# One VectorE multiply in place of two ScalarE activations that normalise the attention result of a head pair

## The chip, the cores and the metric

The kernel runs on one core of a Trainium2 chip. The core has five engines that each take their instructions strictly in the order in which they stand: TensorE (PE in the profile, PEld for its weight loads), VectorE (DVE), ScalarE (ACT), GpSimd (POOL) and SyncE (SP, which here only issues DMAs). They wait for one another by semaphores. The metric is the device time of one execution in microseconds (us); lower is better.

## The reference

The program computes attention with a top-k mask, then a dense layer, then a layer of experts. What matters here is the first part:

```
scores = scale * (q @ k^T)                    # 4 batches, 8 heads, 576 tokens, 64 per head
kth    = 32nd largest of each row
attn   = exp(where(scores >= kth, scores, -1e9) - max)
attn   = attn / (sum(attn) + 1e-9)            # the division of this case
x      = attn @ v                             # then heads side by side: 2304 tokens x 512
h      = softplus(x @ w_in); x2 = h @ w_out   # dense layer, 512 -> 2048 -> 512
out    = gate * (relu(x2 @ w1[e]) @ w2[e])    # each token by its one expert e of 8
```

The kernel does not divide the weights. It multiplies the unnormalised weights by v, with a column of ones beside v so that the sums come out as a 65th column, and divides the result.

## The kernel before, in words

The program has two parts. Part one does the attention, the dense layer and the routing of each token to its expert; part two does the experts.

Attention goes in 72 groups of two score tiles. A score tile is 128 queries (or twice 64, called the tail) of one head against all 576 keys. For a group, TensorE writes scores into two PSUM tiles, `sa` and `sb`, one buffer each (L401); ScalarE copies both to SBUF as `s` (L411, L447); VectorE reads `sb` and `s` and finds the 32 largest values of each row (L441 to L446 fold the row into shorter candidate lists, L451 to L467 pick eight at a time, in place); ScalarE and GpSimd make the masked exponentials `e` (L477 to L479); ScalarE and GpSimd split `e` into two 16-bit halves `p` (L487 to L489); SyncE issues a DMA that transposes `p` into `pT` (L491). `p` has two buffers.

Three groups later `emit_av` multiplies `pT` by v (L506, L508) into the PSUM tile `m`. `m` has one buffer and holds both heads of a pair, each with 64 results and its sum. When the second head is done, VectorE makes `rc`, the reciprocal of the two sums (L530, L532), and the two heads are multiplied by it into `x` (L534). This happens 80 times: 64 times for 128 queries, 16 times for the 64 of a tail. Only then may TensorE write `m` for the next pair. When all four head pairs of some tokens are in `x`, `unit_x` splits it into 16-bit halves (ScalarE L553, GpSimd L554) and transposes it by DMA; the dense layer (L593, L607, L608, L633) runs on it in between the attention groups. The weights of the dense layer are decoded in the first 300 us on ScalarE, VectorE and GpSimd (L243 to L256).

The order on each engine is not written by hand. A scheduler places the instructions by its own estimate of when each can start, with priorities given in the code (`tc.high_priority`), so that a change of one instruction can shift its neighbours on all engines. The matmuls of `emit_av` are to be issued behind the next group's score matmuls (L822). The program holds a second copy of part one for unusual inputs; it does not run here, and it has the same lines.

Of the kernel before, what the change touches and what calls it, by code (L numbers as in the profile page):

```python
# [13 lines left out]
AF = mybir.ActivationFunctionType  # L14
ALU = mybir.AluOpType
# [4 lines left out]
B, H, S, D = 4, 8, 576, 64  # L20
# [176 lines left out]
def part_one(tc, ctx, q, k, v, w_in, w_out, const, ident, before, ones, iota_e, reg_e, wg, ids,  # L197
             ohcum, done, early, table, rows, flags, sums, w_sums, e_sums, kths):
    nc = tc.nc
# [294 lines left out]
    def x_tile(key):  # L494
        if key not in x_t:
            x_t[key] = xp.tile([128, NP, 2, D], F32, name=f"x{key[1]}", bufs=XB if isinstance(key[1], int) else 1)
        return x_t[key]

    def emit_av(m, kind):
        b, hp = pairs[m]  # L500
        v16, sc = pair[m][3:5]
        pT = pt_t.pop((m, kind))
        def products(o, pT, h):
            for r in range(R):
                c = r if r < 5 else r - 5
                nc.tensor.matmul(o[:, h, 0:D + 1], lhsT=pT(r), rhs=v16[:, h, c, 0:D + 1], start=r == 0, stop=r == R - 1)  # L506
                if r < 5:
                    nc.tensor.matmul(o[:, h, 0:D], lhsT=pT(r), rhs=v16[:, h, c, D + 2:], start=False, stop=False)  # L508

        def out_tile():  # L510
            return ps_m.tile([128, 512], F32, name="m")[:, :2 * D + 4].rearrange("p (h c) -> p h c", h=2)

        if kind == "tail":
            o = out_tile()
            p0 = 64 * (b % 2)
            for h in range(2):
                products(o[p0:p0 + 64], lambda r: pT[:, r, h * 64:h * 64 + 64], h)
            xt, ps_ = x_tile((b // 2, "tail%d" % (b // 2))), slice(p0, p0 + 64)
        else:
            t, h = kind  # L520
            if h == 0:
                o_t[m, t] = out_tile()
            o = o_t[m, t]
            products(o, lambda r: pT[:, r, :], h)
            if h == 0:
                return
            del o_t[m, t]
            xt, ps_ = x_tile((b, t)), slice(0, 128)
        rc = sm.tile([128, 2, 1], F32, name="rc")
        nc.vector.tensor_scalar(rc[ps_], o[ps_, :, D:D + 1], ESC * 1e-9,  # L530
                                2.0 ** -X_UP if flags is not None else sc[ps_, 2:3], op0=ALU.add, op1=ALU.mult)
        nc.vector.reciprocal(rc[ps_], rc[ps_])  # L532
        for h in range(2):
            nc.scalar.activation(xt[ps_, hp, h], o[ps_, h, 0:D], AF.Copy, scale=rc[ps_, h])  # L534


    def unit_x(tiles):
# [250 lines left out]
    for i in range(-1, n + LAG):  # L788
# [29 lines left out]
        if j >= 0:  # L818
            with tc.high_priority(offset=A_AV), ExitStack() as behind_scores:
                if i + 1 < n:  # L820

                    behind_scores.enter_context(tc.issue_after(last_qk[0].ins))  # L822
                for x in groups[j]:
                    emit_av(*x)
            for u in units.get(j, []):
                started += 1
                ready.append((u, started))
# [274 lines left out]
```

## Time and profile before

| | us |
|---|---|
| time, median of 3 runs (lowest to highest) | 1096.41 (1095.99 to 1100.68) |
| time of the profiled execution | 1104.11 |
| its span, from the first to the last instruction | 1102.3 |
| its mean granted TensorE clock | 0.925 of full speed |

The profile records each instruction of one execution with its start and its length. "Busy" counts the time in which an engine had an instruction under way; instructions of one engine may overlap, so that the time from one start to the next is often shorter than the length of one. "Idle" times name the instruction whose end released the waiting engine. The chain of waits goes back from the last instruction to what released it, and so on to the start. The profiled execution took 7.7 us more than the median; all sums are made as differences in it and then carried to the median.

### The profile page before, as it was taken

How to read it: one execution, taken by the hardware profiler on the slowest of the kernel's cores; microseconds unless marked ns; L12 is line 12 of the kernel's file. 1: busy time of each engine (PE TensorE's matmuls, PEld its weight loads, DVE VectorE, ACT ScalarE, POOL GpSimd, SP SyncE). 2: the span in 40 equal slices, each digit the busy share in tenths (PEclk: the TensorE clock that was granted, in tenths of full speed). 3: DMA queues.
4: the chain of work that ended last, by engine and by line, in shares of the span. 5: the costliest groups of instructions: out<-in, count | busy, mean ns of one | idle time of the engine just before them, and what ended most of it. 6: DMA issues, size and time to landing. Idle time of an engine off the chain costs nothing.

```text
span 1102.3 us, 22261 instructions
## 1 busy us (share of the span) xinstructions
PE 900.3 (82%) x7146; PEld 664.0 (60%) x7146; DVE 852.6 (77%) x2921; ACT 833.1 (76%) x2026; POOL 603.8 (55%) x631
## 2 busy tenths in 40 slices
PE   1124359675978978799989799998999999999995
PEld 0012246344655655666556566666688899999993
DVE  3898999699966847889889799982445897777774
ACT  4889899798868867989897898994478655555553
POOL 2788898798656756767776877773101011211111
PEclk9976569876988989899999999999999999999998
DMA  7888898776756878867978646644601486676660
GB/s 173 202 200 182 180 205 180 164 159 129 126 77 122 143 122 119 134 76 126 139 153 124 106 79 93 86 80 67 202 1 30 99 252 205 217 245 227 228 222 23
DMA packets 295860, 156.98 MB, mean 142 GB/s; under 512 B 257524, under 2 KB 257652, under 8 KB 295732
## 3 DMA queue, kind: packets, MB, share of 16 engines
q1 hardware_dynamic: 292116, 145.73, 63.1%
q0 software_dynamic: 3616, 9.72, 2.6%
q8 instruction: 58, 0.95, 0.4%
q14 instruction: 70, 0.57, 0.2%
HBM read 77.89 MB, written 11.11 MB: 81 GB/s over the span
## 4 chain that ended last, share of the span: by engine, by line
PE 37%; DMA 19%; ACT 17%; POOL 9%; DVE 8%; issue 5%; SPq 3%; POOLq 0%; ACTq 0%; DVEq 0%
PE h L933 9%; DMA pT<-p 9%; PE y L946 9%; PE h L593 6%; PE y L633 4%; POOL p L489 3%; PE y L630 3%; ACT p L487 3%; POOL e L478 2%; DMA w<-in_moe_w_out_dram 2%; ACT e L479 2%; ACT e L477 2%; DVE mx L467 2%; DMA vn<-in_v_dram 2%; DVE wk L463 1%
## 5 line engine op out<-in xcount | busy, mean ns | idle before, releaser
L593 PE MATMUL h<-xT,w_in_s 128*128 128x256 f16 (+1 forms) x1920 | 231.8, 272 | 18.6 <-DMA xT<-xh 7.4
L633 PE MATMUL y<-w_out_s,g 128*128 128x512 f32 x480 | 233.9, 610 | 2.0 <-ACT g L608 2.0
L593 PEld LDWEIGHTS <-w_in_s 128*128 128x128 f16 x1920 | 177.0, 102 | 86.4 <-issue 53.8
L478 POOL TENSOR_TENSOR e<-s,e 128x576 f32<-128x576 f32 x144 | 204.0, 1432 | 22.1 <-ACT e L477 21.8
L467 DVE MAX8 mx<-wk 128x8 f32<-128x128 f32 (+2 forms) x432 | 201.1, 500 | 0.1
L401 PEld LDWEIGHTS <-q 128*128 128x128 f16 (+1 forms) x640 | 56.2, 109 | 195.7 <-issue 148.5
L489 POOL TENSOR_TENSOR p<-e,p 128x512 f16<-128x512 f32 x144 | 167.3, 1162 | 0.0
L463 DVE MATCH_REPLACE8 wk<-mx,wk 128x128 f32<-128x128 f32 (+1 forms) x432 | 144.4, 340 | 0.0
L487 ACT ACTIVATE p<-e 128x576 f16<-128x576 f32 x144 | 97.9, 683 | 42.1 <-DMA pT<-p 41.3
L401 PE MATMUL sa<-kt,q 128*128 128x256 f16 (+1 forms) x320 | 52.9, 304 | 86.7 <-ACT s L411 35.2
L633 PEld LDWEIGHTS y<-w_out_s,g 128*128 128x128 f32 x480 | 83.4, 194 | 62.4 <-issue 57.4
L913 POOL DMA_INDIRECT out_dram<-ot,idx x19 | 19.6, 1030 | 176.3 <-DVE ot L912 156.5
L479 ACT ACTIVATE e<-e,bias 128x576 f32<-128x576 f32 x144 | 111.0, 772 | 6.1 <-POOL e L478 5.9
L401 PE MATMUL sb<-kt,q 128*128 128x320 f16 (+1 forms) x320 | 63.6, 342 | 63.4 <-ACT s L447 63.4
L933 PEld LDWEIGHTS h<-xT,wf 128*128 128x128 f32 x864 | 111.9, 191 | 5.3 <-ACT wf L894 0.2
L933 PE MATMUL h<-xT,wf 128*128 128x256 f32 x864 | 114.0, 283 | 0.0
L946 PE MATMUL y<-wf,hT 128*128 128x512 f32 x432 | 112.9, 399 | 0.3 <-DVE ds L690 0.3
L477 ACT ACTIVATE e<-s,kths 128x576 f32<-128x576 f32 x144 | 106.2, 770 | 1.2 <-POOL p L489 0.4
L506 PE MATMUL m<-v,pT 128*128 128x65 f16 (+1 forms) x1440 | 96.0, 203 | 8.1 <-ACT xtail L534 6.8
L488 POOL TENSOR_TENSOR p<-e,p 128x64 f16<-128x64 f32 x144 | 45.6, 317 | 96.4 <-ACT p L487 80.9
L506 PEld LDWEIGHTS <-pT 128*128 128x128 f16 (+1 forms) x1440 | 89.5, 107 | 14.2 <-issue 10.9
L441 DVE TENSOR_TENSOR sb<-sb,s 128x256 f32<-128x256 f32 x72 | 30.6, 425 | 73.0 <-ACT s L411 48.9
(204 smaller groups left out, 1885.5 us busy)
## 6 DMA issues: line engine op xcount, KB each, us to landing
w1r<-in_moe_w_dram SPq DMA_DIRECT2D x20, 1024.0 KB, 6.0
w2r<-in_moe_w_dram SPq DMA_DIRECT2D x20, 1024.0 KB, 7.7
w<-in_moe_w_in_dram SPq DMA_DIRECT2D x16, 512.0 KB, 5.1
w<-in_moe_w_out_dram SPq DMA_DIRECT2D x16, 512.0 KB, 4.2
rows<-xr SPq DMA_DIRECT2D x37, 128.2 KB, 2.4
qn<-in_q_dram SPq DMA_DIRECT2D x16, 288.0 KB, 3.4
kn<-in_k_dram SPq DMA_DIRECT2D x16, 288.0 KB, 3.2
vn<-in_v_dram SPq DMA_DIRECT2D x16, 288.0 KB, 3.7
```

The source lines that it names most:

```text
L401: last_qk[0] = nc.tensor.matmul(ps[p0:p1], lhsT=qs[:, h, r0:r1, :].rearrange("p r d -> p (r d)"), rhs=kt[:, k0:k1, cs], start=first, stop= ...
L463: nc.vector.match_replace(out=to, in_to_replace=mx[:, i, 8 * j:8 * j + 8], in_values=src[i], imm_value=NEG)
L467: nc.vector.max(out=mx[:, i, 8 * j + 8:8 * j + 16], in_=src[i])
L478: nc.gpsimd.tensor_tensor(out=e[i], in0=s[i], in1=e[i], op=ALU.subtract)
L479: nc.scalar.activation(e[i], e[i], AF.Exp, bias=bt[:, i], scale=SCORE)
L487: nc.scalar.activation(p16[:, 0:S], e[i], AF.Copy)
L489: nc.gpsimd.tensor_tensor(out=p16[:, S + D:], in0=e[i][:, 0:S - D], in1=p16[:, 0:S - D], op=ALU.subtract)
L506: nc.tensor.matmul(o[:, h, 0:D + 1], lhsT=pT(r), rhs=v16[:, h, c, 0:D + 1], start=r == 0, stop=r == R - 1)
L593: nc.tensor.matmul(hps[:, :n], lhsT=w_in_s[:, c, j, p, o:o + 128], rhs=xT[:, 0:len(u.tiles), r, c, :], start=m == 0, stop=m == 3 * KD - 1)
L633: nc.tensor.matmul(u.y[i], lhsT=g[:, cs], rhs=w_out_s[:, f, :], start=f == 0, stop=f == KF - 1)
L933: nc.tensor.matmul(h, lhsT=w1f[:, a, c, :], rhs=xT[:, b, c, :], start=n == 0, stop=n == 3 * KD - 1)
L946: nc.tensor.matmul(y[i], lhsT=hT[g][:, a, i * 128:i * 128 + 128], rhs=w2f[:, b, :], start=g == 0 and n == 0, stop=g == KF2 - 1 and n == 2)
```

## The change

Two ScalarE instructions (one for each head, 128 x 64 elements from PSUM, scaled by that head's reciprocal) are taken out. One VectorE instruction over both heads (128 x 2 x 64 elements from PSUM, times `rc` repeated along the row) takes their place. It does the same arithmetic.

```
-        for h in range(2):
-            nc.scalar.activation(xt[ps_, hp, h], o[ps_, h, 0:D], AF.Copy, scale=rc[ps_, h])
+        nc.vector.tensor_tensor(out=xt[ps_, hp], in0=o[ps_, :, 0:D],
+                                in1=rc[ps_].to_broadcast([ps_.stop - ps_.start, 2, D]), op=ALU.mult)
```

The new instruction has line 533. In the orders below, names are those of the code (`rc`, `m`, `sb`, `s`, `gt`, `wk`, `xh` as above; `x` with a number is one tile of `x`), and a row is one instruction, or several alike with their count. First VectorE, at the second head pair of the first batch, near the start of the program. Before:

```order
L467 MAX mx<-wk 128x8 x2
L530 TENSOR_SCALAR rc<-m 128x2
L532 RECIPROCAL rc<-rc 128x2
L441 TENSOR_TENSOR sb<-sb,s 128x2x128
L442 TENSOR_TENSOR gt<-sb,s 128x256
L443 TENSOR_TENSOR wk<-sb,gt 128x2x128
```

And in the changed kernel:

```order
L467 MAX mx<-wk 128x8 x2
L530 TENSOR_SCALAR rc<-m 128x2
L532 RECIPROCAL rc<-rc 128x2
L441 TENSOR_TENSOR sb<-sb,s 128x2x128
L533 TENSOR_TENSOR x_922<-m,rc 128x128
L442 TENSOR_TENSOR gt<-sb,s 128x256
L443 TENSOR_TENSOR wk<-sb,gt 128x2x128
```

The multiply stands behind L441, the first instruction of the next group's search, which itself waits for scores. Second, ScalarE, where the first finished tile of `x` is split for the dense layer (with what each row waits for in brackets). Before:

```order
L534 ACTIVATE x_789<-m,rc 128x64 [waits DVE_49,PE_49]
L534 ACTIVATE x_789<-m,rc 128x64
L477 ACTIVATE e<-s,kths 128x576 [waits Activation_49]
L477 ACTIVATE e<-s,kths 128x576 [waits Pool_49]
L243 ACTIVATE xr<-w 128x512 [waits DMAHW2_49]
L247 ACTIVATE w<-w 128x512
L553 ACTIVATE xh<-x_789 128x512 [waits Activation_49]
L447 ACTIVATE s<-sb 128x2x320 [waits DVE_49]
```

And in the changed kernel:

```order
L243 ACTIVATE xr<-w 128x512 [waits DMAHW1_49,Pool_49]
L247 ACTIVATE w<-w 128x512
L476 ACTIVATE kths<-mx 128x2 [waits DVE_49]
L477 ACTIVATE e<-s,kths 128x576 [waits Activation_49]
L477 ACTIVATE e<-s,kths 128x576 [waits Pool_49]
L553 ACTIVATE xh<-x_789 128x512 [waits DVE_49]
L447 ACTIVATE s<-sb 128x2x320 [waits DVE_49,PE_49]
```

The two activations are gone from ScalarE's row, and the split L553, which waited for ScalarE's own work, waits for VectorE.

## Rows read from the trace of the kernel before

**Rows 1.** Busy time by stretch; columns as the first row says.
```profile
core 0: us, PE busy (x) PEld busy (x) DVE busy (x) ACT busy (x) POOL busy (x), PEclk, DMA share, GB/s
55.00:770.00 715.00, 574.08 (x4998) 385.99 (x4999) 599.03 (x2226) 602.99 (x1502) 529.68 (x548) 0.89 0.72 130
770.00:1102.00 332.00, 317.37 (x2118) 273.79 (x2116) 220.69 (x593) 192.95 (x448) 44.69 (x43) 0.99 0.51 162
```
**Rows 2.** Chain that ended last, shares of the whole span by engine.
```profile
PE 37%; DMA 19%; ACT 17%; POOL 9%; DVE 8%; issue 5%; SPq 3%; POOLq 0%; ACTq 0%; DVEq 0%
```
**Rows 3.** The chain from 770 us to the end, by line.
```profile
by line: PE h L933 31.3%; PE y L946 30.2%; PE h L593 11.4%; PE y L630 10.4%; PE y L633 3.1%; PE tp L903 2.5%; PE h L961 1.6%; PE h L667 1.2%; PE y L978 1.0%; PE h L661 0.7%; ACT wf L894 0.4%; issue 0.4%; PE h L688 0.3%; DVE wf L895 0.3%; AC
```
**Rows 4.** Who waited for whom: us in total, times, longest.
```profile
DVE sb L441 <- ACT s L411: 48.9, 23, 11.4
DVE sb L441 <- PE sb L401: 22.9, 10, 8.4
PE sb L401 <- ACT s L447: 63.4, 20, 6.7
ACT p L487 <- DMA pT<-p: 41.3, 19, 8.0
DVE rc L530 <- PE m L506: 23.2, 13, 5.4
ACT x L534 <- DVE rc L532: 7.6, 5, 3.2
```
**Rows 5.** ScalarE's groups by form: line, shapes, count, busy us, mean ns.
```profile
L534 ACT ACTIVATE x<-m,rc 128x64 f32<-128x64 f32 x128 | 32.6, 307 | 10.6 <-DVE rc L532 7.6 <-DVE sf L1011 2.5 <-PE h L593 0.4
L534 ACT ACTIVATE xtail<-m,rc 64x64 f32<-64x64 f32 x32 | 8.1, 303 | 0.2
```
**Rows 6.** ScalarE's timeline around two pairs: start us, us, instruction.
```profile
520.11 0.53 ACT L534 ACTIVATE x<-m,rc 128x64 f32<-128x64 f32 x2
520.50 0.80 ACT L477 ACTIVATE e<-s,kths 128x576 f32<-128x576 f32 x1
...
694.97 0.51 ACT L534 ACTIVATE xtail<-m,rc 64x64 f32<-64x64 f32 x2
695.50 0.70 ACT L447 ACTIVATE s<-sb 128x640 f32<-128x640 f32 x1
```
**Rows 7.** VectorE's groups by form, as Rows 5.
```profile
L441 DVE TENSOR_TENSOR sb<-sb,s 128x256 f32<-128x256 f32 x72 | 30.6, 425 | 73.0 <-ACT s L411 48.9 <-PE sb L401 22.9 <-ACT x2T L663 1.2
L445 DVE COPY wk<-sb 128x128 f32<-128x128 f32 x72 | 20.1, 279 | 0.0
L470 DVE TENSOR_TENSOR flags<-mx 128x16 f32<-128x16 f32 x18 | 15.7, 870 | 0.3
L530 DVE TENSOR_SCALAR rc<-m 128x2 f32<-128x2 f32 x64 | 9.5, 148 | 18.9 <-PE m L506 18.9
```
**Rows 8.** VectorE's timeline inside one search.
```profile
460.95 0.28 DVE L445 COPY wk<-sb 128x128 f32<-128x128 f32 x1
461.15 0.68 DVE L446 TENSOR_TENSOR wk<-sb,s 128x512 f32<-128x512 f32 x1
```
**Rows 9.** Single lines of VectorE: shortest, median and longest instruction in ns.
```profile
L470 DVE TENSOR_TENSOR flags<-mx x18: 177/454/3612, 63.7 to 740.0; 128x16 f32<-128x16 f32 x18
L441 DVE TENSOR_TENSOR sb<-sb,s x72: 404/432/433, 22.4 to 731.6; 128x256 f32<-128x256 f32 x72
```
**Rows 10.** VectorE's timeline where L441 stands between L530 and L532.
```profile
528.34 0.14 DVE L530 TENSOR_SCALAR rc<-m 64x2 f32<-64x2 f32 x1
532.00 0.43 DVE L441 TENSOR_TENSOR sb<-sb,s 128x256 f32<-128x256 f32 x1 [3.51 <-ACT s L411]
532.34 0.14 DVE L532 RECIPROCAL rc<-rc 64x2 f32<-64x2 f32 x1
```
**Rows 11.** Line 534 alone: who waited for it (us, times).
```profile
PE m L506: 8.1, 9
```

## The prediction

> **What bounds the kernel now.** I read the busy times by stretch first. From 55 to 770 us, while attention runs, VectorE is busy 599.0 of 715 us and ScalarE 603.0, both 84%; TensorE is at 574.1 and GpSimd at 529.7 [rows 1]. No engine is full, and the two between which work is moved are equally loaded. After 770 us attention is over, and the changed lines no longer run. The chain shows who sets the end: over the whole span 17% of it is ScalarE and 8% VectorE, 19% DMA [rows 2]. From 770 us on it is matmuls almost alone, with 0.4% for ScalarE and 0.3% for VectorE in the largest groups shown [rows 3], so that nearly all of ScalarE's and VectorE's shares lie before, and the last 332 us should keep their length. Third, the waits. VectorE's largest is at L441, the first step of a search: 48.9 us for ScalarE's copy L411 and 22.9 us for TensorE's scores [rows 4], and TensorE in turn stands 63.4 us in front of `sb` until ScalarE has emptied it with L447 [rows 4]. So ScalarE is late for VectorE more than the other way round. ScalarE's own largest wait in attention is for the transposing DMA of `p`, 41.3 us [rows 4]: there it has nothing to do, and a lighter ScalarE only waits longer.
>
> **What the change removes.** 160 activations on ScalarE, 40.7 us by the two groups (32.6 + 8.1) [rows 5]. Their mean lengths are 307 and 303 ns, so that two one after the other would be 0.61 us, but they overlap: a pair takes 0.53 us, and the next instruction starts 0.39 us after the pair did in the one place and 0.53 us in the other [rows 6]. Times 80 that is 31 or 42 us; I take the middle, 36 us. The Trainium skill (ScalarE: Activation LUTs, "What ACT_TABLE_LOAD costs") says that back-to-back activations overlap by about 93 ns; by it a pair costs less than its two lengths, and the trace agrees, since 0.61 less 0.53 us is 0.08 us. ScalarE also loses 7.6 us of waiting for `rc` [rows 4], and TensorE 8.1 us of waiting for L534 to free `m` [rows 11]; I count neither, since the new instruction puts waits of its own in their place.
>
> **What it adds.** 80 VectorE instructions, each over 128 elements from PSUM. The nearest row is L445, a copy of 128 x 128 elements out of PSUM, 279 ns long [rows 7], whose successor starts 0.20 us after it [rows 8]. 14 of the 80 stand directly behind the reciprocal that they wait for and are charged the whole 0.279 us, 66 stand elsewhere and are charged 0.20 us: 3.9 + 13.2 = 17 us. The lower bound is the short L530 at 148 ns, 80 times, 12 us [rows 7]; the upper one is L470, the only row with an operand repeated along the row, 870 ns mean, 70 us [rows 7]. I keep near L445, because L470 is not long by nature: its shortest is 177 ns and its longest 3612, while L441, which reads PSUM and SBUF as the new instruction does, never leaves 404 to 433 ns [rows 9]. The Trainium skill (GPSIMD Engine Reference, "Specifications") says that GpSimd contends with VectorE for SBUF where a VectorE instruction has two SBUF inputs. L470 has two and is stretched, L441 has one and is not, so the trace agrees; by that rule the new instruction stays short, by the mean of L470 alone it would be a rival, below. [...]
>
> **What it moves.** The scheduler shifts work on all engines after the first head pairs. Counted in the two orders, the progress of the dense layer against attention is alike: with the 40th of the 80 results multiplied both have issued 48 blocks of its first layer, with the last one 122. The transposes and loads stand at nearly the same places in SyncE's queue, the subtractions in GpSimd's. I take nothing for this, and 10 us either way for the range: the longest single waits at L441 are 11.4 and 8.4 us [rows 4], so that one group more or less that comes so badly placed is worth that much. Two waits change hands. TensorE's first matmul into `m` waits for VectorE and not for ScalarE; behind it in TensorE's row stand the dense layer's matmuls and the next scores. And 16 of the 18 splits L553 wait for VectorE, where before ScalarE's own order was enough; behind a split stands for example L447, for which VectorE's next L441 waits. A split costs nothing where the last multiply is long done. As an upper bound each could wait as long as L441 does on average, (48.9 + 22.9) / 33 = 2.2 us [rows 4]: 18 times, 39 us on ScalarE. I take 0, because the multiply stands rows ahead of the split in the order.
>
> **The sum.** Not every us of an engine is on the chain. ScalarE's 17% of 1102.3 us is 187 us, 0.31 of its 603 busy us; VectorE's 8% is 88 us, 0.15 of its 599 [rows 1, 2]. 36 us less on ScalarE at 0.31 are -11.2 us; 17 us more on VectorE at 0.15 are +2.6 us. Together -8.6 us: 1104.1 becomes 1095.5 for the profiled execution, and the median 1096.4 becomes 1088.
>
> **The rivals.**
> - *Hidden anyway.* ScalarE's relief goes into its 41.3 us of waiting for the transposes [rows 4], whose DMAs come no sooner. 19% of the chain being DMA speaks for it [rows 2]; that only part of these waits is at the places where the activations stood speaks against it. The gain is nothing, VectorE's 2.6 us remain, and the shifted order is left as the only other difference: 1097 us.
> - *The multiply held behind L441.* In the new order L441 stands between L530 and the multiply 17 times; before, it stood between L530 and the reciprocal 10 times, and then `rc` came late: at 528.34 us L530 is done, L441 waits 3.51 us for ScalarE, and L532 starts only at 532.34 [rows 10]. Until the multiply is through, `m` is not free, and TensorE holds its row. At 2.2 us each, the 7 further places give +15 us on TensorE. It decides as soon as these waits are on TensorE's path in most of the places; against it speaks that the 10 old ones cost TensorE little, 8.1 us for all waits on L534 [rows 11]. With the gain of 8.6 us off: +6.8, 1103 us. Without that gain, 1111 us, the upper part of the range.
> - *Stretched like L470.* 70 us on VectorE in place of 17. The 116 us in which VectorE is idle in attention [rows 1] could hold it, but they are waits in the middle of searches. With all of it on the path, less the 36 us of ScalarE: +34, 1130 us.
> - *ScalarE was the bound.* All 36 us come back, as VectorE's 48.9 us of waiting for L411 shrink [rows 4]; VectorE gives back its 2.6: -33, 1063 us. Two engines equally busy speak against it.
> - That the change doesn't do what it says: the 160 activations are gone from ScalarE's order, and the 80 multiplies stand in VectorE's. There is no such case to price.
>
> **How the numbers follow.** I give my forecast 0.46, the hidden gain 0.22, the held multiply 0.22, the stretched one 0.04 and the bound ScalarE 0.06. A difference under 0.5%, 5.5 us, can't be told from none here: faster is below 1090.9 us, slower above 1101.9. The forecast's own range is 1077 to 1098: the chain's shares could be wrong by half, and the order adds noise. Two thirds of it lie below 1090.9 and nearly one third between. Faster: 0.31 of the forecast, 0.06 of the bound ScalarE, 0.04 of the hidden gain and 0.03 of the held multiply, 0.44. Slower: 0.15 of the held multiply, 0.04 of the stretched, 0.05 of the hidden gain through its order, 0.02 of the forecast, 0.26. The rest, 0.30, is no difference. The range reaches down over a part of the bound ScalarE and up over both prices of the held multiply: 1072 to 1111 us.
>
> **What would show it.** L533 should be 0.28 us long (0.20 to 0.35), 80 times, 22 us by its group. ScalarE should be busy some 40 us less in attention, VectorE's waits at L441 for L411 should shrink from 48.9 us, and ScalarE's wait for the transposes should grow by less than ScalarE lost. The end of attention should come some 9 us earlier, and the last 332 us be as long as before. If the transposes' wait grows by 30 us or more, the gain was hidden; if TensorE waits for L533 much over the 8.1 us that it waited for L534, the multiply is held; if L533 is 0.5 us or longer in the mean, it is stretched. My forecast is wrong if attention ends later with L533 short and TensorE not waiting for it: then the shifted order, or VectorE's extra 17 us at full weight, cost more than ScalarE's relief is worth.

## The result, and the profile after

The changed kernel takes 1068.7 us (median of 4 runs, 1066.5 to 1074.1) against 1098.6 us (1096.0 to 1103.7) for the kernel before, on the same chip: a ratio of 0.973, 95% interval 0.970 to 0.977. That is 30 us faster, 3.5 times the predicted gain of 8.6 us, and below the predicted range. The profiled execution took 1068.5 us with a span of 1066.8. The two profiled executions lie 35.6 us apart, some 6 us more than the medians, so that the times read from the two traces below add up to 35 us and not to 30.

The granted TensorE clock is not the cause. It was 0.938 of full speed in the profiled execution after and 0.925 before; but thirteen executions of the kernel before, timed beside the experiments, had a clock of 0.934 to 0.943 and took 1091.8 to 1101.7 us.

Busy time by stretch, cut where attention ends:

```profile
core 0: us, PE busy (x) PEld busy (x) DVE busy (x) ACT busy (x) POOL busy (x), PEclk, DMA share, GB/s
55.00:735.00 680.00, 561.37 (x4998) 378.88 (x4999) 606.31 (x2306) 572.94 (x1342) 528.35 (x548) 0.91 0.73 137
735.00:1066.00 331.00, 317.47 (x2118) 273.88 (x2116) 220.75 (x593) 192.97 (x448) 44.42 (x43) 0.99 0.50 162
```

Against [rows 1] the last part is 331 us as before (332), and attention is 35 us shorter (680 against 715). ScalarE has lost 160 instructions and 30 us. VectorE has gained 80 instructions and only 7.3 us: over the whole span the new ones, which overlap their neighbours, add 13.1 us to its busy time, and its other instructions take 5.7 us less, L470 alone 4.7. The chain's shares have moved from ScalarE to VectorE [rows 2] (and the transposes of `p`, part of DMA, from 9% of the span to 4%):

```profile
PE 40%; DMA 17%; DVE 14%; ACT 13%; POOL 8%; issue 4%; SPq 3%; POOLq 0%; ACTq 0%; DVEq 0%
```

The waits that answer to [rows 4] (waiting engine and line, who ended the wait, us in total, times, longest):

```profile
PE sb L401 <- ACT s L447: 66.2, 24, 7.2
DVE sb L441 <- ACT s L411: 28.6, 19, 3.2
DVE rc L530 <- PE m L506: 20.6, 12, 4.5
ACT p L487 <- DMA pT<-p: 20.1, 18, 4.1
DVE sb L441 <- PE sb L401: 17.7, 5, 8.6
```

VectorE waits 20 us less for ScalarE's copy L411, and the longest single wait there fell from 11.4 to 3.2 us. What does not fit the prediction is the fourth row: a lighter ScalarE should have waited longer for the transposes, and it waits 20.1 us, half of the 41.3 us before. Something other than ScalarE's load made the transposes come in time (experiment 1 shows what).

The new instruction itself is as estimated (line, shapes, count, busy us, mean ns, idle before it; L470 stands with it for the last section), and its neighbour starts 0.20 us after it, as L446 does after L445 [rows 8]:

```profile
L470 DVE TENSOR_TENSOR flags<-mx 128x16 f32<-128x16 f32 x18 | 11.0, 610 | 0.1
L533 DVE TENSOR_TENSOR x<-m,rc 128x128 f32<-128x128 f32 x64 | 17.8, 279 | 0.5
L533 DVE TENSOR_TENSOR xtail<-m,rc 64x128 f32<-64x128 f32 x16 | 4.5, 283 | 0.3
```

```profile
461.17 0.28 DVE L533 TENSOR_TENSOR x<-m,rc 128x128 f32<-128x128 f32 x1
461.37 0.41 DVE L443 TENSOR_TENSOR wk<-sb,gt 128x256 f32<-128x256 f32 x1
```

TensorE's wait for it, from the answer on line 533 alone, is in the place of the 8.1 us of [rows 11]:

```profile
  PE m L506: 6.3, 4
```

To see where the 30 us arise I marked, in both timelines of VectorE, the start of the first instruction (L441) of each group's search. The groups are counted from 0:

| group | before | after | difference |
|---|---|---|---|
| 9 | 117.2 | 114.6 | -2.6 |
| 18 | 228.6 | 224.1 | -4.5 |
| 27 | 317.6 | 304.9 | -12.7 |
| 30 | 351.2 | 331.3 | -19.9 |
| 33 | 377.6 | 358.4 | -19.2 |
| 36 | 424.3 | 389.7 | -34.6 |
| 48 | 532.0 | 500.5 | -31.5 |
| 69 | 716.5 | 685.1 | -31.4 |

A relief of 0.4 us per group would give a straight line. Instead 30 of the 31 us come between groups 18 and 36, in steps, and behind group 36 nothing is gained. In the kernel before ScalarE stands still four times for over 4 us in that stretch (ScalarE's timeline; in brackets the idle time ahead of the instruction and what ended it):

```profile
308.40 0.68 ACT L487 ACTIVATE p<-e 128x576 f16<-128x576 f32 x1 [7.95 <-DMA pT<-p]
...
334.22 0.68 ACT L487 ACTIVATE p<-e 128x576 f16<-128x576 f32 x1 [4.55 <-DMA pT<-p]
...
393.10 0.68 ACT L332 ACTIVATE junk<-vn 128x576 f16<-128x576 f32 x1 [6.65 <-DMA vn<-in_v_dram]
...
421.38 0.68 ACT L487 ACTIVATE p<-e 128x576 f16<-128x576 f32 x1 [5.65 <-DMA pT<-p]
```

24.8 us in all. (L332 sums up a v tile that is to be prepared; L487 may not write `p` until an earlier `p` has been transposed.) The third shows how such a stall travels: L411 stands behind it on ScalarE, and VectorE's next search begins 11.37 us late, the longest wait at L441 in [rows 4]:

```profile
396.57 0.43 DVE L441 TENSOR_TENSOR sb<-sb,s 128x256 f32<-128x256 f32 x1 [11.37 <-ACT s L411]
```

After the change ScalarE has two waits of over 3 us between 200 and 440 us, 8.5 us in all, both for a staging buffer (L362):

```profile
375.36 0.68 ACT L362 ACTIVATE st<-kn 128x576 f16<-128x576 f32 x1 [3.31 <-DMA q<-st]
...
397.81 0.68 ACT L362 ACTIVATE st<-kn 128x576 f16<-128x576 f32 x1 [5.20 <-DMA q<-st]
```

What stands behind the first stall is seen in SyncE's queue, before:

```profile
288.14 1.14 SPq L698 DMA_DIRECT2D rows<-xr  x2
291.45 1.57 SPq L491 DMA_TRANSPOSE pT<-p  x1
293.12 1.19 SPq L714 DMA_DIRECT2D rows<-xr  x2
294.47 17.47 SPq L491 DMA_TRANSPOSE pT<-p  x3
```

and after:

```profile
281.47 1.14 SPq L698 DMA_DIRECT2D rows<-xr  x2
285.22 1.30 SPq L491 DMA_TRANSPOSE pT<-p  x1
286.62 0.53 SPq L714 DMA_DIRECT2D rows<-xr  x1
287.32 1.31 SPq L491 DMA_TRANSPOSE pT<-p  x1
288.69 0.61 SPq L714 DMA_DIRECT2D rows<-xr  x1
```

L714 writes zeros over rows of a scratch tensor. The second of the two is large; by the issues of that stretch (KB each, median us to landing):

```profile
rows<-xr SPq DMA_DIRECT2D x1, 1154.2 KB, 8.9
```

Before, both stand ahead of the transpose of the next `p`, and that transpose (the first of the three in the last row) then takes 5.03 us in the queue where the ones around it take 1.3 to 1.8, and releases ScalarE some 14 us after its issue; after, one transpose slips in between. The Trainium skill (DMA: Bandwidth & Descriptors, "Queues, rings and completion order") says that on each DMA engine the descriptors are taken in ring order; the two queues agree with it, as the transpose issued behind the large write is the late one.

### The profile page after: what moved, and what is told of

Its sections match the earlier page's. It is cut to its first block, busy times and chain, and to the rows that moved or that the text cites. A ratio compares the mean times of both kernels' runs of the same rounds, so it can differ in the third digit from the quotient of the medians.

```text
span 1066.8 us, 22144 instructions
## 1 busy us (share of the span) xinstructions
PE 887.7 (83%) x7146; PEld 656.9 (62%) x7146; DVE 860.0 (81%) x3001; ACT 802.9 (75%) x1866; POOL 602.2 (56%) x631
## 4 chain that ended last, share of the span: by engine, by line
PE 40%; DMA 17%; DVE 14%; ACT 13%; POOL 8%; issue 4%; SPq 3%; POOLq 0%; ACTq 0%; DVEq 0%
PE h L933 9%; PE y L946 8%; PE h L593 8%; PE y L633 6%; DMA pT<-p 4%; PE y L630 3%; DVE mx L467 3%; DMA w<-in_moe_w_in_dram 3%; DMA kt<-st 2%; POOL p L489 2%; DVE wk L463 2%; DMA q<-st 2%; POOL e L478 2%; DMA w<-in_moe_w_out_dram 2%; ACT e L479 2%
## 5 line engine op out<-in xcount | busy, mean ns | idle before, releaser
L633 PE MATMUL y<-w_out_s,g 128*128 128x512 f32 x480 | 230.5, 604 | 7.4 <-ACT g L608 7.2
L593 PE MATMUL h<-xT,w_in_s 128*128 128x256 f16 (+1 forms) x1920 | 225.5, 267 | 13.3 <-ACT w_in_s L255 5.3
L593 PEld LDWEIGHTS <-w_in_s 128*128 128x128 f16 x1920 | 173.5, 100 | 72.4 <-issue 42.2
L487 ACT ACTIVATE p<-e 128x576 f16<-128x576 f32 x144 | 97.3, 680 | 20.9 <-DMA pT<-p 20.1
L946 PEld LDWEIGHTS y<-wf,hT 128*128 128x128 f32 x432 | 76.7, 189 | 13.4 <-DVE ds L690 0.3
```

The costliest lines, as they stand in the source:

```text
L593: nc.tensor.matmul(hps[:, :n], lhsT=w_in_s[:, c, j, p, o:o + 128], rhs=xT[:, 0:len(u.tiles), r, c, :], start=m == 0, stop=m == 3 * KD - 1)
L633: nc.tensor.matmul(u.y[i], lhsT=g[:, cs], rhs=w_out_s[:, f, :], start=f == 0, stop=f == KF - 1)
L946: nc.tensor.matmul(y[i], lhsT=hT[g][:, a, i * 128:i * 128 + 128], rhs=w2f[:, b, :], start=g == 0 and n == 0, stop=g == KF2 - 1 and n == 2)
```

## The experiments

All but four kernels below hold every instruction to a written order: the scheduler's list of a kernel, or one put together from two of them. In the programs so built every engine's order is that of the list, but for the changes named. "Old order" is that of the kernel before, "new order" that of the changed kernel. All ratios are to the kernel before in the same runs, with 95% intervals.

**1. The exchange and the order apart.** *new_in_old_order*: the new operation in the old order, the multiply right behind its reciprocal. *old_in_new_order*: the two activations in the new order, where the multiply had been dispatched.

> The new multiply, with every other instruction of the part that runs held in the order of the kernel before; the multiply stands right behind its reciprocal. Theory A (the exchange of the operations itself gives the gain, as ScalarE was what the others waited for): 0.973 to 0.980 of the time before. Theory B (the gain is the new order that the scheduler made, above all between 284 and 424 us, where 20 to 29 of the 35 us arise): 0.992 to 1.000.

> The two activations, with every other instruction held in the order of the changed kernel; the pair stands on ScalarE where the changed kernel dispatched the multiply. Theory A: 0.995 to 1.005 of the time before, the gain gone. Theory B: 0.973 to 0.985, the gain kept.

Measured: 1.003 [1.001, 1.006] and 0.988 [0.985, 0.992]. The first lies above the ranges of both theories, the second between them. In the old order the exchange gains nothing; in the new order 13 us are there without it, and the exchange adds some 16 (0.988 to 0.973). It is the order that makes the transposes come in time: with both activations still on ScalarE, the wait for them in the new order is (old_in_new_order; its profiled execution took 1074.3 us, 12 less than its median)

```profile
ACT p L487 <- DMA pT<-p: 18.3, 17, 3.7
```

The same holds for ScalarE's waits of over 3 us between 200 and 440 us. In the old order they come to 24.8 us with the old operation and 22.0 with the new one (new_in_old_order), in the new order to 11.5 with the old one and 8.5 with the new.

**2. Which engine's load counts in the new order.** *act_filler* keeps the multiply and gives ScalarE two dead activations in place of those removed:

```
+        jk = stg.tile([128, 2, D], F16, name="jk")
+        for h in range(2):
+            nc.scalar.activation(jk[ps_, h], ident[ps_, 0:D], AF.Copy, scale=rc[ps_, h])
```

*dve_twice* does the multiply twice:

```
+        nc.vector.tensor_tensor(out=jk[ps_], in0=o[ps_, :, 0:D],
+                                in1=rc[ps_].to_broadcast([ps_.stop - ps_.start, 2, D]), op=ALU.mult)
```

> The changed kernel in its own order, and on ScalarE two activations more for each pair, over 128 x 64 elements of SBUF with a scale read from rc, whose result nobody reads: ScalarE's 36 to 42 us are back, VectorE keeps the multiply, and m is still freed by VectorE. Theory A: 0.99 to 1.005 of the time before, since ScalarE's time was the gain. Theory B: 0.973 to 0.985. If it was who frees m that counted, 0.973 too.

> The changed kernel in its own order, with the multiply done twice, the second time into a tile that nobody reads: 16 to 22 us more on VectorE, on which m is freed 0.2 us later. By the prediction's share of VectorE in the chain (0.15): +2.6 us, 0.976 of the time before. If VectorE's time is at full weight: +16 us, 0.988.

Measured: 0.986 [0.983, 0.990] and 0.977 [0.974, 0.981]. 35 us more on ScalarE (busy 837.7 against 802.9) cost 14 us, 0.4 us each; with them come 6.9 us in which ScalarE stands before a dead activation until `rc` is ready. The result lies between the ranges of the two theories. 14.5 us more on VectorE (874.5 against 860.0) cost 4 us, and the interval overlaps that of the changed kernel. So in this order ScalarE's load has a price. VectorE's is below full weight, since 0.988 lies outside the interval, but cannot be told from none, nor, us for us, from ScalarE's.

**3. Place of the multiply, place of the gain.** *old_dispatch*: the new operation in the old order, the multiply where the first activation had been dispatched. *window_new*: the same with only the instructions between the searches of groups 17 and 37 in the new order. *window_old*: the new order, with that stretch in the old one. *window_new_late*: only groups 28 to 37 in the new order.

> The new operation with every other instruction in the order of the kernel before; the multiply stands on VectorE where that order had dispatched the first of the two ScalarE operations (some instructions of other work between it and its reciprocal), no longer right behind its reciprocal as in new_in_old_order (1.0031). If new_in_old_order was flat only because VectorE stood at the multiply waiting for its reciprocal, this run gives the exchange its price: about -14 us, ratio 0.985 to 0.990. If in the old order the freed ScalarE time is worth nothing, wherever the multiply stands, the ratio is 0.997 to 1.004 and the waits of ScalarE's L487 for the transposes stay near 37 us.

> The new operation; the order of before, except that the instructions between the search of group 17 and that of group 37 (about 220 to 430 us; 2,430 of 12,216 instructions) stand in the order that the changed kernel has. If the gain is made by the order of that stretch: ratio 0.972 to 0.982, the waits of L487 for the transposes near 20 to 25 us, and the start of group 36 near 390 us. If the gain is spread over the whole order, or made by ScalarE's lighter load everywhere: 0.990 to 1.003.

> The complement: the new operation in the new order, except that the same stretch (groups 17 to 37) stands in the old order. If the stretch makes the gain: 0.995 to 1.005, with the start of group 36 near 419 to 424 us. If the gain is spread: 0.973 to 0.985.

> As window_new with only groups 28 to 37 in the new order (about 325 to 430 us). Of the 35 us, by the starts of the searches, 12 had come by group 27 and 22 came between 27 and 36. If the stretches add up: ratio 0.980 to 0.986. If the later stretch profits only where the earlier one has run ahead: 0.993 to 1.003.

Measured: 1.004 [1.001, 1.007], 0.992 [0.989, 0.995], 0.995 [0.993, 0.997] and 1.000 [0.998, 1.003]. The place of the multiply is not it; in old_dispatch the wait for the transposes, expected near 37 us, came to 51.1. Putting the stretch back into the old order takes 24 of the 29 us away; alone in the old order it gives 13 us against old_dispatch. It gave more at first: group 36 started 26 us before that of the kernel before, but group 69 only 20, and from the last search to the end window_new takes 377 us, where before takes 371 and after 365. The last nine groups alone give 4 us against old_dispatch, with intervals that overlap. So most of the gain needs the order of that stretch, but it is not a sum of pieces. My expectation of 0.972 to 0.982 for window_new was wrong.

**4. SyncE's queue alone.** In *sp_four* the new operation runs in the old order, and only SyncE's queue is changed, at four places, to what stands there in the new one. The first and the last:

```
 L714 DMA rows<-xr 64x513
-L714 DMA rows<-xr 576x1x513
 L491 DMA_TRANSPOSE pT<-p_3430
+L714 DMA rows<-xr 576x1x513
...
+L491 DMA_TRANSPOSE pT<-p_4856
 L322 DMA vn<-in_v_dram
-L322 DMA kn<-in_k_dram
 L698 DMA rows<-xr
-L698 DMA rows<-xr
-L491 DMA_TRANSPOSE pT<-p_4856
 L491 DMA_TRANSPOSE pT<-p_4862
+L322 DMA kn<-in_k_dram
+L698 DMA rows<-xr
```

*sp_all* has all of that queue's stretch in the new order, *old_op_sp_four* is the kernel before with the four places changed, and *sp_undone* is the changed kernel with the four places put back.

> As old_dispatch (new operation, order of before), except that SyncE's queue alone stands in the new order at four places, 26 of its 623 entries: the 1,154 KB zero write (L714) goes behind one transpose in place of ahead of it; a kt transpose goes ahead of two pT transposes; one k load and one row write go behind two pT transposes and the v load; and one pT transpose goes ahead of a v load, the other ahead of a k load and a row write. In the traces of the order of before, ScalarE's L487 and L332 stand 8.0, 4.6, 6.7 and 5.7 us behind these transfers (at 300, 330, 386 and 416 us). Theory Q, that these collisions in the queue are where the new order gains: the four stalls shrink by 12 to 20 us in all, ratio 0.984 to 0.992. Rival, that the order on the computing engines gains and the queue only follows: the stalls stay or are replaced, ratio 1.000 to 1.005.

> As sp_four with all of SyncE's queue between 285 and 470 us in the new order (91 entries), the other four engines as in before. Theory Q: like sp_four or better, 0.978 to 0.990. Rival (the other engines' order): 1.000 to 1.005.

> The reverse: the changed kernel with its own order, in which SyncE's queue alone stands in the order of before at the same four places. Theory Q: the stalls of ScalarE at L487 and L332 come back and it loses 12 to 20 us, ratio 0.984 to 0.992. Rival: 0.972 to 0.977, as the changed kernel.

> The kernel before, with both ScalarE operations and its own order, in which SyncE's queue alone takes the four new places. If the queue's gain is there without the exchange: 0.984 to 0.992. If ScalarE needs the time that the exchange frees before the queue can help: 0.995 to 1.003.

Measured: sp_four 0.998 [0.995, 1.001], sp_all 1.000 [0.997, 1.003], sp_undone 0.985 [0.981, 0.989], old_op_sp_four 0.996 [0.993, 0.999]. In the new order four places of one queue are worth 13 us, 0.985 against 0.973. The first stall is back (7.31 us at 301 us), and so is the last, longer than ever (ScalarE's timeline, then SyncE's queue, of sp_undone):

```profile
407.16 0.68 ACT L487 ACTIVATE p<-e 128x576 f16<-128x576 f32 x1 [11.57 <-DMA pT<-p]
```

```profile
392.43 0.34 SPq L322 DMA_DIRECT2D vn<-in_v_dram  x1
395.61 0.33 SPq L322 DMA_DIRECT2D kn<-in_k_dram  x1
396.06 1.11 SPq L698 DMA_DIRECT2D rows<-xr  x2
397.21 3.38 SPq L491 DMA_TRANSPOSE pT<-p  x2
400.69 5.73 SPq L368 DMA_TRANSPOSE q<-st  x2
```

Two loads of 288 KB and two row writes stand ahead of the two transposes, as at 408 us in the kernel before; the next `p` is held 11.57 us. Over the whole run two of its waits are those of the kernel before, although its ratio is 0.985, so that they alone do not give the time:

```profile
DVE sb L441 <- ACT s L411: 49.1, 22, 12.1
ACT p L487 <- DMA pT<-p: 42.2, 19, 11.6
```

In the old order the same four places give 6 us with the new operation (0.998 against 1.004) and 5 with the old one. sp_four lies between the ranges of theory Q and its rival. Its trace shows what is in the way: the stalls at the transposes shrank (8.0 to 3.75 us at the first, the last gone, the second as before), but ScalarE also stands at two sums over v tiles that have not landed. The first of them is the third stall of the kernel before (6.65 us there, 5.07 in old_dispatch); the second is new. The four come to 20.6 us, against 21.8 in old_dispatch:

```profile
382.99 0.68 ACT L332 ACTIVATE junk<-vn 128x576 f16<-128x576 f32 x1 [5.15 <-DMA vn<-in_v_dram]
...
408.23 0.68 ACT L332 ACTIVATE junk<-vn 128x576 f16<-128x576 f32 x1 [7.06 <-DMA vn<-in_v_dram]
```

**5. ScalarE's order, and what is left.** *act_two* is sp_four with two sums L332 moved down ScalarE's row. *six_moves* is the changed kernel with six instructions that wait there for a transfer (four L362, two L332) moved down by 3 to 8 places.

> As sp_four (new operation, order of before, four places of SyncE's queue in the new order: 0.998), and on ScalarE two sums over a v tile (L332 junk<-vn, which nothing reads soon) stand 10 and 12 instructions later, so that the loads have landed when they come up. Theory: ScalarE stands in order behind late transfers, in whatever instruction meets them, and this is what the old order loses; the two stalls (5.2 and 7.1 us) go, and the ratio is 0.985 to 0.993. Rival: the 12 us come back at another instruction, and the ratio stays at 0.996 to 1.001.

> The changed kernel in its own order, except that six instructions of ScalarE that wait there for a transfer (L362 at 336, 375, 398 and 507 us, L332 at 245 and 417 us; 16.2 us of waits in all) stand 3 to 8 instructions later. Theory: about half of these waits is won, 4 to 10 us, ratio 0.964 to 0.970. Rival: they are covered, or come back elsewhere, 0.971 to 0.978.

Measured: 0.996 [0.993, 0.998] and 0.974 [0.971, 0.978]. Of the two stalls act_two only took away the second (7.06 to 0.66 us): I had moved the sums of two neighbouring pairs of heads, and one of them was not the one that stalled at 383 us, which still waits 6.28 us. 0.996 against 0.998 is inside the intervals, so that the run neither confirms nor refutes its theory. six_moves gains nothing: the waits for the staging buffer (16.9 us in the changed kernel, 9.3 for q and 7.6 for k) are no longer among its largest, and that for the transposes has grown in their place from 20.1 to 27.3 us (ScalarE's waits in attention):

```profile
ACT p L487 <- DMA pT<-p: 27.3, 18, 5.1
```

**6. Other orders.** The scheduler made its own order here, with one number changed in both kernels: `A_PREP = 140` in place of 150 (*prep140*), or `A_SC = 95` in place of 100 (*sc95*).

> The kernel before with one number changed, A_PREP = 140 in place of 150, the lead that the scheduler's priorities give to the preparation of the next pair of heads; nothing else is changed, but the scheduler then orders the main block anew. If an order from any cause moves the time by about as much as the change did: outside 0.995 to 1.005, as low as 0.985 or as high as 1.015. If the order of the changed kernel was special: 0.996 to 1.004.

> The changed kernel with the same A_PREP = 140. If the exchange gains in any order that the scheduler makes for it: 0.970 to 0.985, and 10 us or more under before_prep140. If most of the gain was the luck of one order: 0.985 to 1.000, and within 8 us of before_prep140.

> The kernel before with A_SC = 95 in place of 100, the lead of the scores in the scheduler's priorities; nothing else is changed. If orders differ by about 1 per cent among themselves: anywhere from 0.980 to 1.012, most likely outside 0.997 to 1.003.

> The changed kernel with A_SC = 95. If the exchange gains nothing by itself and the order decides: within 12 us of before_sc95, on either side, and above 0.980. If the exchange gains as in the original pair: 20 us or more under before_sc95.

Measured: 1091.0 and 1090.6 us (0.992 [0.990, 0.995] and 0.993 [0.990, 0.996]) with A_PREP, 1091.9 and 1091.9 us (0.995 [0.993, 0.997] and 0.995 [0.993, 0.998]) with A_SC. In neither pair does the change move the time clear of the intervals, and a new order by itself moved the kernel before by 5 to 8 us. Here the two kernels of a pair have different orders, so that exchange and order are not apart: a gain of the one could be lost by the other. With A_SC = 95 the waits look like the case that the prediction called hidden: VectorE's wait for ScalarE shrinks, and ScalarE's for the transposes grows. Before and then after:

```profile
DVE sb L441 <- ACT s L411: 47.3, 21, 7.5
ACT p L487 <- DMA pT<-p: 25.1, 11, 6.4
```

```profile
ACT p L487 <- DMA pT<-p: 34.8, 15, 4.8
DVE sb L441 <- ACT s L411: 40.8, 19, 7.2
```

None of the runs is faster than the changed kernel.

## Why the prediction was wrong, point by point

- **What moved: the failed step.** The prediction looked at the orders, found that "the transposes and loads stand at nearly the same places in SyncE's queue", and went on: "I take nothing for this, and 10 us either way for the range". 71 of that queue's 623 entries had moved. The old operation in the new order gains 13 us (0.988), and four places of SyncE's queue are worth 13 us in the new order (sp_undone). The two 13 us are two measurements, and neither run shows that they are the same 13: without the exchange the four places were timed in the old order alone, where they are worth 5. "Nearly the same" by counting is no argument where one transpose stands ahead of or behind a 1,154 KB write. The trace of before had shown the price: L487's longest wait, 8.0 us [rows 4], was one of the four stalls, and I had not asked what stood ahead of it in the queue.
- **What ScalarE's time is worth.** One weight, 0.31, was taken from the chain's shares for 36 us. Measured, it depends on the order. In the new one ScalarE's 35 us cost 14, a weight of 0.4, from which 0.31 cannot be told. In the old one the exchange gained nothing (1.003, 1.004), where 8.6 us were forecast, nor did the change gain with either priority. What differs between the old and the new order is where the relief goes: in the old order L487's wait grows from 41.3 to 51.1 us (old_dispatch), in the new one it is 20.8 with the filler and 20.1 without, and VectorE's wait for L411 shrinks from 39.4 to 28.6. That this is the whole reason is argued, not shown: in new_in_old_order, no faster, both waits are lower than before (36.7 and 35.2 us), and with A_PREP = 140 the wait for L411 shrinks by 22.8 us, that for the transposes grows by only 4.8, and the time is the same.
- **The removed and added work: nearly right.** ScalarE is busy 30 us less in attention, where 36 stood in the sum and some 40 were said as a sign: 80 pairs come to 0.38 us each, the lower of the two distances in [rows 6]. At 0.31 the 6 us are worth 2, so that this is not the miss. L533 is 0.28 us long, 22.3 us by its two groups (22 were said), and its neighbour starts 0.20 us later; it adds 13 us to VectorE's busy time, where 17 stood in the sum. VectorE's weight of 0.15 stands against 4 us for 14.5 (dve_twice), which cannot be told from it.
- **The waits.** L441's for L411 shrank as said. L487's was to grow by less than ScalarE lost, and halved: the order's work, not the load's, as 18.3 us with both activations in the new order show. The last part kept its length, and attention ended 35 us earlier, not 9.
- **The rivals.** Held behind L441: no, TensorE waits 6.3 us for L533. Stretched like L470: no, L533 runs from 260 to 295 ns. ScalarE the bound, 1063 us: nearest to the measured number, and not the cause, since in the old order the same relief gains nothing. Hidden anyway, 1097 us (by its own terms, 1096.4 + 2.6, it is 1099): in time, what the exchange comes to by itself in the old order; with the other priorities that is not shown. No rival let the order gain more than 10 us.

Put together, of the 30 us some 13 are the order without the exchange, and some 16 are ScalarE's relief, which this order turns into time and the old one does not. What in the order sets the transposes right is shown for four places of SyncE's queue. Why ScalarE's relief counts in the one order alone stays open.

## What to carry to other kernels

Where a scheduler reorders the program, time a change twice: with the order held to the old one, and with one or two other priorities. If the ratio changes with them, the gain belongs to the order, at least in part, and can be lost or won again by the next edit. Read the DMA queue around the longest waits entry by entry: here a write of 1,154 KB that nobody waited for stood ahead of a transpose that the pipeline waited for, and ScalarE stood 8.0 us. Then time the moved entry, since the same four places were worth 13 us in one order and 5 to 6 in the other.

## What was not expected of the hardware

L470, which does the same work in every kernel, has a mean of 870 ns before [rows 7] and 610 ns after, because other instructions of the kernel stand elsewhere in time. The two traces show which: those of GpSimd. Nine of their 36 L470 start with no GpSimd instruction under way and take 163 to 188 ns. Of the other 27, all but one end 0.04 to 0.09 us after the end of a GpSimd instruction that ran beside them. One of the long ones, in the kernel before, outlasts two such instructions (VectorE's timeline, then GpSimd's):

```profile
526.03 2.38 DVE L470 TENSOR_TENSOR flags<-mx 128x16 f32<-128x16 f32 x1
```

```profile
525.86 1.40 POOL L478 TENSOR_TENSOR e<-s,e 128x576 f32<-128x576 f32 x1
527.23 1.15 POOL L554 TENSOR_TENSOR xh<-x,xh 128x512 f16<-128x512 f32 x1
```

And, of the program and not of the hardware, a change of one priority by 5 or 7% moves the kernel by 5 to 8 us, about as much as the whole forecast of this case.
